# Gate and up of a gated layer: both pairs of token chunks by seven products in eight feature groups, instead of one pair

## The chip, the cores and the metric

The kernel runs on one core of a Trainium2 chip. Its engines have queues of their own and run side by side: TensorE (PE) multiplies into PSUM, VectorE (DVE), ScalarE (ACT) and GpSimd (POOL) work element by element, and SyncE (SP) issues DMAs. ACT and POOL can issue DMAs too. GpSimd reads and writes SBUF only. Each engine works through its instructions in the order in which the program gives them to it, and a waiting instruction holds up those behind it. The metric is the time of one execution on the device, in microseconds (us).

## The reference: what is computed

A sequence of 2048 tokens of width 640 is normalized; one branch is a dilated, sliding attention (32 heads of 20, 8 positions at distance 2), the other a bilinear gated layer with 1536 features, and their product is added to the input:

```
xn = layernorm(x)
s  = attention(xn @ wqkv) @ wo            # 8 keys per token: t, t-2, ..., t-14
h  = (xn @ w_gate) * (xn @ w_up)          # 640 -> 1536, twice
g  = silu(h @ w_down)                     # 1536 -> 640
out = x + s * g
```

The change is in the two products that make h.

## The kernel before, in words

**Precision.** Every matmul operand is split into a high part (rounded to the format that PE takes in one pass) and a low part (the rest). A product is then three passes: high x high, high x low, low x high (`ALL3`, line 109). A split is an ACT copy for the high part and a subtraction on POOL or DVE for the low part (`split`, line 104).

**Tiling.** The 2048 tokens are four chunks of 512 (`CH`); xT[c] holds chunk c transposed, as a high and a low tile of five blocks of 128 input features. The 1536 features of gate and up are twelve groups f of 128. gate_up (line 583) does one group for one chunk: 15 matmuls for gate, 15 for up, an ACT copy of gate, a DVE product h = gate x up, a store of h to DRAM (h_scr). Groups 0 and 1 are done this way for all chunks at the start, mixed with the first qkv products.

**Seven products.** For f = 2 to 11, `group(f)` (line 1215) takes chunks 0 and 1 together: gate and up of two chunks, over four of the five input blocks, are a 2 x 2 by 2 x 2 block product, done with seven block products instead of eight. It needs sums of weights (S1 to S4, made by `w_add` on POOL and split by `w_split`) and sums of activations (T1 to T4, made by `differences` on POOL during the qkv products). T4 takes the place of a part of xT[1]. The fifth input block is added by three matmuls each to four of the products (`FIVE`). That is 7 x 6 + 4 x 3 = 54 matmuls. Partial results are held by four ACT copies into the five-buffer tile gh (`hold`); DVE does gate_b, gate_a and up_a, POOL up_b and h_b. Chunks 2 and 3 are then done plainly (`gate`, `up`, `plain`): 60 matmuls, two ACT copies, two DVE products.

**Order of work.** The order in each engine's queue is the order of the calls, written out by hand. At the start (lines 1024 to 1104), tiles of 128 tokens are normalized on DVE: `moments_q` (batch statistics, line 315), `scales` (lines 322 to 328, a chain of small DVE operations on 128 x 4 elements), `spread` (a matmul on PE that stands in the middle of a gate_up, line 330), and `trans_q` (line 339): four applies (line 279), a 32 x 32 transpose (line 347), the high part on ACT (line 350) and the low part on DVE (line 351, put off by one tile). The qkv products of a tile (line 409) need its high and low parts. Attention is a Python generator (line 442): `advance` takes steps from it against a credit that each piece of PE work adds, so DVE and POOL instructions of attention are laid between those of the feature groups. Its products read one operand from PSUM (q_two and weights), its additions of terms run on POOL (line 482). `finish_piece` (line 623) lays the put-off DVE work of the last gate_up or group. begin_last (line 1350) lays all of attention that is left and loads wo; it comes in group 10. After group 11 the output projection and the down projection follow.

Of the kernel before, what the change touches and what calls it, by code (L numbers as in the profile page):

```python
# [19 lines left out]
P = 128  # L20
# [7 lines left out]
CH = 512  # L28
# [16 lines left out]
PACE = 1.0  # L45

# [7 lines left out]
def kernel(  # L54
# [174 lines left out]
    o_scr = dr.tile([DIL, NQ, NE, P, QC], F32, name="o_scr")  # L229
    h_scr = dr.tile([NT, P, KF, P], F32, name="h_scr")  # L230
# [124 lines left out]
    ORDER = [0, 1, 2, 3, 4, 6, 5, 7, 8, 10, 9, 11]  # L355
# [86 lines left out]
    def attention():  # L442
# [9 lines left out]
        before, late, loaded = None, [], set()  # L452
# [18 lines left out]
        def values(w):  # L471
# [5 lines left out]
            t = terms[:, w % 2, :NE * c] if w else y  # L477
# [4 lines left out]
            return NE * c * cost, lambda: eng.tensor_add(y, y, t)  # L482

        ring[:] = [q_one, "g", "u"]
        for n, u in enumerate(ORDER + [None]):
# [14 lines left out]
            for j in PAIRS:  # L500
# [6 lines left out]
                if before is not None:  # L507
                    cost, add = values(j or 1)
                    if j:
                        add()  # L510
                    else:
                        late.append(add)
                    yield cost
# [4 lines left out]
                if before is not None:  # L518
                    cost, add = values(j + 1 if j else 0)
                    if j:  # L520
                        add()
                    else:
                        late.pop()()
                    yield cost
# [23 lines left out]
            before = u, e, st([P, NE, c], "pk" if n in (7, 9, 11) else "o", 1)  # L548
# [13 lines left out]
    running = []  # L562

# [498 lines left out]
    low_parts()  # L1062
    finish_piece()
# [10 lines left out]
    gate_up(0, 1, amid=(lambda: spread(8),))  # L1074
    nc.scalar.activation(st([P, 1], "exp", 1), eps_t, AF.Exp)
# [3 lines left out]
    trans_q(10)  # L1079
    gate_up(1, 1, amid=(lambda: spread(12),))  # L1080
# [10 lines left out]
    trans_q(13)  # L1091
    trans_q(14)
    gate_up(0, 2)
    trans_q(15)
    low_parts()
    made.add(0)
# [10 lines left out]
    tt, tw, steps = [], {}, []  # L1107
# [3 lines left out]
    def t_unit(j, a, k):  # L1111

        if j == "T4":
            return xT[1][a][:, k, :]
        n, i = T_UNIT[j, a, k]
        while len(tt) <= n:
            tt.append(slot([P, 3, CH]))
        return tt[n][:, i]
# [3 lines left out]
    def differences(k):  # L1122
# [3 lines left out]

        def parts(j, y):
            nc.scalar.activation(t_unit(j, 0, k), y, AF.Copy)
            nc.gpsimd.tensor_sub(t_unit(j, 1, k), y, t_unit(j, 0, k).bitcast(F32))

        def minus(c, y):
            z = st([P, CH], "gh", 5)
            nc.gpsimd.tensor_sub(z, x(c[0], 0, c[1]), y)
            yield
            nc.gpsimd.tensor_add(z, z, x(c[0], 1, c[1]))
            yield
            return z

# [430 lines left out]
```

## Time and profile before

| what | value |
|---|---|
| median of 3 runs | 750.93 us (750.75 to 752.1) |
| the profiled execution | 750.62 us |
| its span, first to last instruction | 748.7 us |
| PE busy | 742.9 us, 4102 matmuls |
| DVE, POOL, ACT busy | 598.5, 423.8, 275.8 us |
| first matmul of group 2, of group 11 | 271.8, 504.4 us |

The span is shorter than the execution by what lies before the first and after the last instruction. Busy time counts instructions of an engine, not those that issue DMAs. A line such as "L279 DVE TENSOR_SCALAR" names the line of the kernel, the engine and the operation; "out<-in" gives the tiles. In the timeline a row has its start and its length in us, a count of merged instructions, and in brackets the idle time before it with what ended it. The granted clock of PE is 1.0 in nearly the whole span.

### The profile page before, as it was taken

The numbers are of one execution on the slowest core, as the hardware profiler recorded it, in microseconds if no ns is written. First come the engines' busy times: TensorE is split into PE (matmuls) and PEld (weight loads), VectorE is DVE, ScalarE is ACT, GpSimd is POOL, SyncE is SP. The second block draws the span as 40 slices with busy tenths as digits, with TensorE's granted clock in tenths as the row PEclk, the third lists the DMA queues.
The fourth block names the chain that finished last, engine by engine and source line by source line (L and its number), as shares of the span: only waits on it lengthen the run. The fifth ranks groups of instructions, "written<-read, shape, count | busy, mean of one in ns | idle before, by whom it ended". The sixth has DMA issues, their size and how long they took to land.

```text
span 748.7 us, 11061 instructions
## 1 busy us (share of the span) xinstructions
PE 742.9 (99%) x4102; PEld 678.5 (91%) x4102; DVE 598.5 (80%) x753; ACT 275.8 (37%) x513; POOL 423.8 (57%) x341
## 2 busy tenths in 40 slices
PE   9999999999999999999999999999999999999997
PEld 7989989988999998888888888888999999999997
DVE  7899897699687888978897887434998787777775
ACT  5334223232232332332232322235466564444442
POOL 6100329797698989895988798865659900000000
PEclk9999999999999999999999999999999999999999
DMA  9464352957627554636263522453667665555534
GB/s 330 155 201 118 119 167 81 280 179 231 178 84 224 181 169 129 205 92 186 76 183 88 154 63 56 146 159 91 175 186 214 210 237 190 190 190 190 190 106 141
DMA packets 99747, 122.48 MB, mean 164 GB/s; under 512 B 22280, under 2 KB 73988, under 8 KB 99694
## 3 DMA queue, kind: packets, MB, share of 16 engines
q1 hardware_dynamic: 82094, 107.53, 46.0%
q10 hardware_dynamic: 17600, 14.26, 5.9%
q8 instruction: 32, 0.52, 0.3%
q14 instruction: 21, 0.17, 0.1%
HBM read 78.34 MB, written 42.57 MB: 161 GB/s over the span
## 4 chain that ended last, share of the span: by engine, by line
PE 99%; DVE 0%; POOL 0%; ACT 0%; issue 0%; POOLq 0%
PE u L116 13%; PE g L116 13%; PE q L409 10%; PE q L852 8%; PE u L409 8%; PE g L1250 8%; PE g L409 8%; PE u L852 6%; PE u L1250 5%; PE g L852 3%; PE e L852 3%; PE q L1250 3%; PE q L116 2%; PE q L989 2%; PE u L989 1%; PE e L409 1%
## 5 line engine op out<-in xcount | busy, mean ns | idle before, releaser
L482 POOL TENSOR_TENSOR o<-o,t 128x960 f32<-128x960 f32 (+1 forms) x63 | 128.5, 2039 | 37.5 <-DVE o L479 26.4
L107 POOL TENSOR_TENSOR s<-wraw,s 128x640 fp32r<-128x640 f32 (+4 forms) x67 | 88.3, 1330 | 85.5 <-ACT s L106 82.6
L116 PE MATMUL g<-xc,s 128*128 128x512 f32 (+1 forms) x435 | 100.5, 382 | 0.0
L116 PE MATMUL u<-xc,s 128*128 128x512 f32 (+1 forms) x435 | 100.4, 382 | 0.0
L479 DVE TENSOR_TENSOR t<-e,kv 128x960 f32<-128x960 f32 (+1 forms) x84 | 87.1, 1038 | 13.6 <-POOL o L482 13.5
L505 DVE TENSOR_TENSOR t<-q,kv 128x1920 f32<-128x1920 f32 (+1 forms) x48 | 92.4, 1926 | 4.5 <-DMA kv<-qkv_scr 3.8
L116 PEld LDWEIGHTS u<-xc,s 128*128 128x128 f32 x435 | 79.7, 188 | 15.7
L116 PEld LDWEIGHTS g<-xc,s 128*128 128x128 f32 x435 | 79.7, 188 | 15.5
L515 DVE TENSOR_REDUCE lg<-t 128x96 f32<-128x1920 f32 (+1 forms) x48 | 92.3, 1923 | 0.1
L409 PE MATMUL q<-s,xc 128*128 128x360 f32 (+1 forms) x450 | 82.7, 334 | 0.0
L409 PEld LDWEIGHTS q<-s,xc 128*128 128x128 f32 x450 | 74.8, 188 | 4.0 <-POOL s L107 0.8
L409 PE MATMUL u<-s,xc 128*128 128x360 f32 (+1 forms) x360 | 65.8, 334 | 0.0
L409 PEld LDWEIGHTS u<-s,xc 128*128 128x128 f32 x360 | 60.3, 187 | 2.3
L409 PE MATMUL g<-s,xc 128*128 128x360 f32 (+1 forms) x330 | 61.5, 337 | 0.0
L106 ACT ACTIVATE s<-wraw 128x768 fp32r<-128x768 f32 (+6 forms) x68 | 41.9, 631 | 50.4 <-PE u L116 30.0
L409 PEld LDWEIGHTS g<-s,xc 128*128 128x128 f32 x330 | 55.7, 187 | 2.6
L852 PE MATMUL q<-xc,s 128*128 128x320 f32 x342 | 55.5, 309 | 0.0
L852 PEld LDWEIGHTS q<-xc,s 128*128 128x128 f32 x342 | 51.5, 188 | 0.0
L482 POOL TENSOR_TENSOR pk<-pk,t 128x960 f32<-128x960 f32 (+1 forms) x18 | 35.9, 1996 | 12.7 <-DVE pk L479 7.2
L1250 PE MATMUL g<-xc,s 128*128 128x512 f32 x150 | 37.3, 389 | 0.0
L815 DVE TENSOR_TENSOR s<-s,s 128x768 fp32r<-128x768 f32 x29 | 28.3, 975 | 10.1 <-ACT s L811 10.1
L1222 ACT ACTIVATE gh<-g 128x512 f32<-128x512 f32 x30 | 17.9, 598 | 46.2 <-PE g L1250 46.2
(341 smaller groups left out, 1342.5 us busy)
## 6 DMA issues: line engine op xcount, KB each, us to landing
h_scr<-gh SPq DMA_DIRECT2D x48, 256.0 KB, 2.5
wraw<-in_wgu SPq DMA_DIRECT2D x11, 640.0 KB, 4.6
kv<-qkv_scr SPq DMA_DIRECT2D x14, 480.0 KB, 5.1
qkv_scr<-s ACTq DMA_DIRECT2D x18, 360.0 KB, 3.3
t<-h_scr SPq DMA_DIRECT2D x8, 768.0 KB, 7.0
kv<-qkv_scr SPq DMA_DIRECT2D x14, 367.5 KB, 5.8
s_scr<-gh SPq DMA_DIRECT2D x16, 320.0 KB, 4.2
gh<-s_scr SPq DMA_DIRECT2D x16, 320.0 KB, 4.3
```

The costliest lines, as they stand in the source:

```text
L106: nc.scalar.activation(hi, raw, AF.Copy)
L107: eng.tensor_sub(lo, raw, hi.bitcast(F32))
L116: nc.tensor.matmul(acc, a, b, start=first and n == 0, stop=last and n == len(runs) - 1)
L409: nc.tensor.matmul(p, xT[(r * NE + i) // TPC][a][:, k, t0:t0 + P], wq[m][b][k], start=n == 0, stop=n == len(runs) - 1, skip_group_check=ac ...
L479: nc.vector.tensor_mul(t.rearrange("p (n d) -> p n d", d=DH), e[:, :, w].unsqueeze(2).to_broadcast([P, NE * nh, DH]), v)
L482: return NE * c * cost, lambda: eng.tensor_add(y, y, t)
L505: nc.vector.tensor_mul(t, q, k)
L515: nc.vector.tensor_reduce(out=lg[:, :, j:j + 2].rearrange("p n a -> p a n"), in_=t.rearrange("p a (n d) -> p a n d", d=DH), op=ALU.add, ax ...
L815: nc.vector.tensor_sub(hT[m][:, 1], h_raw[n][name], hT[m][:, 0].bitcast(F32))
L852: nc.tensor.matmul(p, y[:, i, k], wd_t[name][k][:, l], start=new and r == 0, stop=r == len(runs) - 1, skip_group_check=True)
L989: nc.tensor.matmul(b, y, w, start=new and r == 0, stop=r == len(runs) - 1, skip_group_check=True)
L1250: nc.tensor.matmul(y, w, x, start=j in (0, 1, 5) and r == 0, stop=r == len(runs) - 1, skip_group_check=True)
```

## The change

For f = 3 to 10 the second pair of chunks, now the pair 2 and 3 first and then 0 and 1, is done by seven products too, with the same sums of weights: `group(f, 2)` and `group(f, 0, 1)`. In f = 2 the seven products take pair 2/3 and the plain ones chunks 0 and 1; f = 11 stays as it was. For this:

- The sums T1 to T4 of pair 0/1 are made early. early_sums(0) stands after the qkv products of tiles 4 and 5, early_high(0) behind gate_up(0, 1), early_sums(1) after tile 10, early_high(1) after tile 13. Their tiles lie in buffers that held x; from there they go to DRAM (t_scr, e_scr). The part of xT[3] that T4 of pair 2/3 overwrites is kept in DRAM too.
- POOL's queue issues the loads: t_scr in groups 2 and 3, e_scr into xT[1] in group 3 and back into xT[3] after group 10.
- `differences` makes the sums of pair 2/3, in eleven POOL operations per k instead of thirteen.
- In the groups on pair 2/3 with f from 3 (VEC), up_b and h_b run on DVE instead of POOL; on pair 0/1 they stay on POOL. The splits and sums of the next group's weights are laid at given products of the second group (two_places). The up weights' first half (A21) is no longer split where no plain product needs it; the gate weights use the tile pk, so attention's results always use the tile o, and its first term goes to a tile of terms.
- The last rows of attention units run in the order 11, 9, 10, and the last qkv part takes r = 1 first.
- begin_last comes at the first product of group 10's second half; split_wo and sums_wo, which stood in group 10, come there and in group 11.

```
+    def early_sums(k):
+        r0, r1, a, b = early_t[:4]
...
+        for out, add, u, v in ((r0, 1, x(1, 0, 0), x(1, 1, 0)), (r1, 1, x(1, 0, 1), x(1, 1, 1)),
+                               (a, 0, r0, x(0, 0, 0)), (a, 0, a, x(0, 1, 0)), (b, 0, r1, a), (r0, 0, r1, r0),
+                               (r1, 0, x(0, 0, 1), b), (r1, 1, r1, x(0, 1, 1))):
+            (nc.gpsimd.tensor_add if add else nc.gpsimd.tensor_sub)(out, u, v)
+
+    def early_high(k):
+        r0, r1, a, b = early_t[:4]
+        for n, (j, y) in enumerate((("T1", a), ("T2", b), ("T3", r0), ("T4", r1))):
+            hi = early_t[4 + n].bitcast(F32R)
+            nc.scalar.activation(hi, y, AF.Copy)
+            nc.gpsimd.tensor_sub(y.bitcast(F32R), y, hi.bitcast(F32))
+            for l, t in enumerate((early_t[4 + n], y)):
+                nc.sync.dma_start(t_scr[:, T2_UNIT[j, l] + k] if j != "T4" else e_scr[l][:, k], t)
...
     qkv(0, 0, 4)
     qkv(0, 0, 5)
     low_parts()
+    early_sums(0)
     finish_piece()
     moments_q(8, 4)
...
     scales(12)
     gate_up(0, 1, amid=(lambda: spread(8),))
+    early_high(0)
     nc.scalar.activation(st([P, 1], "exp", 1), eps_t, AF.Exp)
     trans_q(8)
     trans_q(9)
     finish_piece()
     trans_q(10)
+    early_sums(1)
     gate_up(1, 1, amid=(lambda: spread(12),))
...
     trans_q(13)
+    early_high(1)
     trans_q(14)
     gate_up(0, 2)
     trans_q(15)
     low_parts()
+    for a in range(2):
+        nc.sync.dma_start(e_scr[2 + a], xT[3][a][:, 0:2, :].bitcast(F32))
...
-    def group(f):
+    def group(f, c0=0, second=0):
...
+        eng = nc.vector if c0 and f >= VEC else nc.gpsimd
...
         def up_b():
-            nc.gpsimd.tensor_add(kept[1], kept[1], kept[4])
+            eng.tensor_add(kept[1], kept[1], kept[4])
 
         def h_b():
-            nc.gpsimd.tensor_mul(kept[2], kept[2], kept[1])
-            store_h(f, 1, kept[2])
+            eng.tensor_mul(kept[2], kept[2], kept[1])
+            store_h(f, c0 + 1, kept[2])
...
+            if f < f1 and f + 1 not in wf_raw:
+                load_wf(f + 1)
...
+            if (second, n) in places:
+                places[second, n](f)
...
-            advance(PACE * len(runs) * 0.184)
+            advance(PACE * len(runs) * (GROUP_RATE if two(f) else 0.184))
...
+    beside.update({(f0, 1, 0): lambda: begin_last(), (f0, 1, 3): lambda: split_wo(0),
+                   (f1, 0, 1): lambda: (split_wo(1), sums_wo(), load_pair(1))})
...
+    two_places = {(0, 5): sums("S1"), (0, 6): sums("S2"), (1, 0): sums("S3"), (1, 1): sums("d5", "S4"),
+                  (1, 2): splits("G"), (1, 4): splits("S"), (1, 5): splits("R"), (1, 6): splits("U")}
...
     for f in range(2, f1):
...
+        places.clear()
+        if not two(f):
...
+            continue
+        places.update(two_places)
+        if f == F_TWO:
+            places.update({(0, n): lambda f, n=n: load_late(n) for n in range(4)})
+        group(f, 2)
+        group(f, 0, 1)
+    places.clear()
+    load_e(3, 0, 2)
+    load_e(3, 1, 3)
...
     group(f1)
```

Here VEC = 3, GROUP_RATE = 0.184 and F_TWO = 3; f0 is 10, f1 is 11, and two(f) is true for f = 3 to 10.

More of the change, by code (lines that the diff above doesn't have):

```diff
@@ L45 @@
 PACE = 1.0
+VEC = 3
+GROUP_RATE = 0.184
 def tile_column(s):
@@ L507, in attention @@
                 if before is not None:
[L508 to L512, printed above, removed]
+                    cost, add = values(j)
+                    add()
                     yield cost
```

191 lines of the change are left out of this document (109 added, 82 removed).

## The prediction

> **What bounds the kernel now.** I read the page first (busy shares, chain), then the windows for two stages, then single instructions in the timeline.
>
> ```profile
> span 748.7 us, 11061 instructions
> ...
> PE 742.9 (99%) x4102; PEld 678.5 (91%) x4102; DVE 598.5 (80%) x753; ACT 275.8 (37%) x513; POOL 423.8 (57%) x341
> ...
> PE 99%; DVE 0%; POOL 0%; ACT 0%; issue 0%; POOLq 0%
> ```
>
> TensorE (PE) is the bound from end to end: the chain that ended last is 99% PE. So a matmul that is removed is worth its whole pitch, and a wait that reaches PE anywhere costs its whole length. The profiled execution took 750.62 us, 1.92 us more than its span; the median of the runs is 750.93. I sum against 750.62. Differences under about 0.2% (1.5 us) can't be told from no change here.
>
> The windows show two stages that the change touches, [40, 60] and the feature groups f = 3 to 9 ([297.64, 478.52]; columns: length, then busy us of PE, PEld, DVE, ACT, POOL):
>
> ```profile
> 40.00:60.00 20.00, 20.00 (x103) 17.43 (x102) 18.81 (x60) 6.05 (x17) 0.00 (x0) 1.00 0.64 200
> ...
> 297.64:478.52 180.88, 180.88 (x799) 149.78 (x798) 149.69 (x141) 49.52 (x79) 153.16 (x113) 1.00 0.41 121
> ```
>
> In the first, VectorE (DVE) is 94% busy and GpSimd (POOL) idle; in the second DVE is at 83% and POOL at 85%.
>
> **Removed: 48 matmuls.** A feature group now costs PE 54 matmuls of 512 columns for the pair done by seven products and 60 for the two plain chunks. One turn of the loop is the time from one group's start to the next:
>
> ```profile
> 297.64 1.52 PE L1250 MATMUL g<-xc,s 128*128 128x512 f32 x6
> ...
> 323.48 0.84 PE L1250 MATMUL g<-xc,s 128*128 128x512 f32 x3
> ```
>
> That is 25.84 us for 114 matmuls, 0.2267 us each. For f = 3 to 10 the 60 become 54: 8 x 6 x 0.2267 = **10.9 us** less. A doubled turn is 108 x 0.2267 = 24.48 us. f = 2 and 11 keep their 114 (the pairs only swap in f = 2).
>
> **Added early: 24 POOL operations beside a full DVE.** early_sums has 8 operations of 512 columns per k, early_high 4 more (and 4 on ACT), for k = 0 and 1: 24 in all on POOL. The like of them, and POOL's idle time up to the split of the next weights, are
>
> ```profile
> 86.66 4.40 POOL L107 TENSOR_TENSOR s<-wraw,s 128x1080 fp32r<-128x1080 f32 x3 [60.05 <-ACT s L106]
> ...
> 109.52 1.29 POOL L1141 TENSOR_TENSOR gh<-xc,xc 128x512 f32<-128x512 f32 x1
> ```
>
> So 24 x 1.3 = 31 us fit into 60 us of idle POOL. By POOL's own time they are free. The question is what DVE does meanwhile. These rows are DVE operations with both inputs in SBUF, with POOL idle (507.28) and busy (526.56 and 528.27), and small ones and a normalization:
>
> ```profile
> 507.28 0.43 DVE L939 TENSOR_TENSOR kv<-kv,wraw 128x256 f32<-128x256 f32 x1
> ...
> 526.21 1.75 POOL L107 TENSOR_TENSOR xc<-o,xc 128x640 fp32r<-128x640 f32 x1
> 526.56 1.68 DVE L939 TENSOR_TENSOR t<-t,s 128x256 f32<-128x256 f32 x1
> ...
> 527.91 1.75 POOL L107 TENSOR_TENSOR s<-t,s 128x640 fp32r<-128x640 f32 x1
> 528.27 1.67 DVE L940 TENSOR_TENSOR t<-s,t 128x256 f32<-128x256 f32 x1
> ```
> ```profile
> 8.40 0.96 POOL L107 TENSOR_TENSOR s<-wraw,s 128x360 fp32r<-128x360 f32 x1
> ```
> ```profile
> 9.01 0.70 DVE L279 TENSOR_SCALAR t<-t,mv,r 128x640 f32<-128x640 f32 x1
> ...
> 17.26 0.61 DVE L279 TENSOR_SCALAR t<-t,mv,r 128x640 f32<-128x640 f32 x1
> ...
> 23.76 2.85 POOL L107 TENSOR_TENSOR s<-wraw,s 128x256 fp32r<-128x256 f32 x4
> ...
> 24.52 0.71 DVE L261 TENSOR_SCALAR lg<-mvo 128x4 f32<-128x4 f32 x1
> ...
> 25.34 0.58 DVE L273 TENSOR_TENSOR lg<-lg 128x4 f32<-128x4 f32 x1
> ```
>
> An operation of 0.43 us becomes 1.68: it ends 0.28 us after POOL's operation ends (526.21 + 1.75 = 527.96), and the next one waits for POOL's next. One DVE operation gets through per POOL operation. Even 4 columns take 0.71 instead of 0.17 us (the 0.17 is below, at 45.73). L279 with POOL in flight until 9.36 ends at 9.71, so its data seem to pass after POOL's end; uncovered, 640 columns take 0.61 us. So the applies, the low parts and the little tensor operations of the scales wait; batch statistics, 32x32 transposes and operations with an input in PSUM do not.
>
> The Trainium skill, page "SBUF — State Buffer", section "Who interferes with whom", says the same: GpSimd and VectorE share a port pair under an exclusive lock, a two-input operation in SBUF or a two-port mode needs it, and who comes second blocks for the whole instruction. By that rule, this trace agrees.
>
> *Stall A, at spread(8).* early_sums(0) can start when the low part of tile 7 ends (40.17 + 0.83 = 41.0):
>
> ```profile
> 40.17 0.83 DVE L351 TENSOR_TENSOR xc<-s,xc 128x640 fp32r<-128x640 f32 x1 [0.81 <-ACT xc L350]
> ...
> 45.73 0.17 DVE L261 TENSOR_SCALAR lg<-mvo 128x4 f32<-128x4 f32 x1
> ...
> 46.25 0.16 DVE L273 TENSOR_TENSOR lg<-lg 128x4 f32<-128x4 f32 x1
> 46.45 0.16 DVE L274 TENSOR_TENSOR lg<-lg 128x4 f32<-128x4 f32 x1
> ...
> 47.05 0.19 DVE L327 TENSOR_TENSOR lg<-mro,lg 128x32 f32<-128x32 f32 x1
> ```
> ```profile
> 44.01 3.56 PE L116 MATMUL g<-xc,s 128*128 128x512 f32 x15
> 47.40 0.36 PE L333 MATMUL e<-lg,lg 128*128 128x32 f32 x2
> ```
>
> Its eight operations end at about 41.0 + 8 x 1.29 = 51.3. scales(8) begins at 45.65, in the middle, and has five or more operations that wait (L261, L273, L274, L275, L276), one per POOL operation: they reach 51.3 before L327 runs, which so ends near 51.7 and not at 47.24. PE's spread (L333) stands in PE's queue between the gate and the up half and starts at 47.40, with no slack behind L327. PE stalls 51.8 - 47.4 = **4.4 us**.
>
> *Stall B, at tiles 8 to 11.* An ACT copy of 512 columns and a DMA issue on SP cost
>
> ```profile
> L1222 ACT ACTIVATE gh<-g 128x512 f32<-128x512 f32 x30 | 17.9, 598 | 46.2 <-PE g L1250 46.2
> ```
> ```profile
> L1212 SPq DMA_DIRECT2D h_scr<-gh x40: 359/376/534, 291.2 to 532.4; - x40
> ```
>
> Behind stall A ACT makes the four high parts of early_high(0) (4 x 0.6 us, ahead of the table load and of tile 8's copy), POOL its four low parts, then, once the store out of r0 has landed, early_sums(1). DVE meanwhile turns tiles 8 to 11 for the qkv products that PE does next (rows from 52.69: scales(12), a tile's applies, low part, transpose and high part, and PE's first four products of that row of tiles):
>
> ```profile
> 52.69 0.19 DVE L327 TENSOR_TENSOR lg<-mro,lg 128x32 f32<-128x32 f32 x1
> ...
> 57.91 1.16 DVE L279 TENSOR_SCALAR s<-s,lg 128x160 f32<-128x160 f32 x4
> 58.20 2.56 PE L409 MATMUL e<-s,xc 128*128 128x360 f32 x15
> 58.99 0.82 DVE L351 TENSOR_TENSOR xc<-s,xc 128x640 fp32r<-128x640 f32 x1
> 59.72 0.84 DVE L347 STREAM_TRANSPOSE s<-s 128x640 f32<-128x640 f32 x1
> 60.60 0.74 ACT L350 ACTIVATE xc<-s 128x640 fp32r<-128x640 f32 x1 [2.41 <-DVE s L347]
> 60.60 2.56 PE L409 MATMUL u<-s,xc 128*128 128x360 f32 x15
> ...
> 63.01 4.96 PE L409 MATMUL q<-s,xc 128*128 128x360 f32 x30
> ```
>
> A tile is four applies, a low part and a transpose, 2.8 us; PE takes a tile in 2.4 us and is 1 to 2 us behind. With POOL busy each apply costs one POOL operation (1.3 us), so a covered tile takes about 4 x 1.35 + 2 x 0.85 = 7 us. Walked through by that rule, from DVE free at 57.4 (scales(12), which ends at 52.9, 4.5 later): tile 8 is ready at 63.4 (PE wants it at 62.6), tile 9 at 66.2, the low part of 9 at 73.3 (wanted at 67.8), tile 10 at 75.0, tile 11 at 79.0; POOL's twelve operations are over at 76. The fourth product starts at 79.0 and not at 65.4 (63.0 + 2.4): 13.6 us late, of which 4.4 are stall A. **Stall B is 9.2 us.** Bounds: 0, and 12 x 1.2 = 14. I take the walk. The last four POOL operations (early_high(1), tiles 14 and 15) fall behind gate_up(0, 2), 6.8 us of PE work that needs none of them: 0.
>
> **Added in the doubled groups.** The plain chunks' two ACT copies and two DVE products become four ACT copies, three DVE operations, and an addition and a product (up_b, h_b) on POOL or, for pair 2/3 from f = 3 on (VEC), on DVE.
>
> ```profile
> L1225 DVE TENSOR_TENSOR gh<-gh,u 128x512 f32<-128x512 f32 x5 | 3.4, 683 | 4.7 <-PE u L1250 2.8 <-issue 1.9
> ```
> ```profile
> L1228 POOL TENSOR_TENSOR gh<-gh,gh 128x512 f32<-128x512 f32 x5 | 6.5, 1294 | 0.0
> ```
> ```profile
> 478.90 2.27 POOL L482 TENSOR_TENSOR pk<-pk,t 128x960 f32<-128x960 f32 x1 [2.16 <-DVE t L479]
> ```
>
> DVE today: 149.69 / 7 = 21.4 us a turn, of which 5 x 0.68 = 3.4 are the groups' and 18.0 attention's. The pacing gives attention 108 x 0.184 = 19.9 credits a turn against 54 x 0.184 + 4 x 2.8 = 21.1, so 16.9 us. New: 16.9 + 6 x 0.68 + two operations with both inputs in SBUF, 0.7 each plus a wait of some 0.9 behind a POOL that is 85% busy = 24.2 us of 24.48. DVE is full. With half a microsecond of waits a turn it falls behind by some tenths per turn, for six turns, until attention ends; the five gh buffers (a hold needs the store of the group before it to have landed) pass a lag beyond some 3 us on to PE. I take **2 us**; bounds 0 and, if DVE holds a turn at the old length, 6 x 1.36 = 8.2. POOL stays near 85%; its weight splits are now due within a few products of the last use, which is in the same bound. ACT, 7 us a turn, has room for 1.2 more.
>
> **At nothing.** The 26 new DMAs (18 on SP, 8 on POOL) meet DMA engines 41% busy (the share in the window above) and are needed 10 us or more after issue; if late, the first product on T2 waits a few us, once. On SP the early stores wait for POOL, and behind them stand the h stores of two gate_up calls (five gh buffers, two used per call) and the load of the next qkv weights, which are split at 85: covered. POOL issues eight loads, an operation that no row here shows: between 0 and SP's issue time, 0.38 us each. The Trainium skill, "DMA: Bandwidth & Descriptors", section "SWDGE vs HWDGE vs iDMA", has GpSimd's DMAs built in software; no run here shows a price. Attention keeps its number of products and additions; two POOL operations per k fall away from differences, off the path. At the end attention is over at 481.2 (478.90 + 2.27, its last POOL addition) and begin_last comes near 482.6, then wo has 5.4 us to land: 0, at most 2.
>
> **Sum.** 750.6 - 10.9 + 4.4 + 9.2 + 2.0 = **755.3 us**.
>
> **Rivals.** (1) *The early work hides* (faster). If POOL's operations let the short DVE operations pass, or run where DVE has statistics and transposes, the early stalls shrink. Decisive is what one POOL operation costs the path: 13.6 us are 18 or so operations at 0.75 us; under (10.9 - 2) / 18 = 0.5 us each the kernel wins. For it: the statistics before 45 us don't wait. Against: no DVE slack there, 18.81 of 20 us. With stall A alone 746.1; with neither 741.7. (2) *DVE bounds the doubled groups*: their gain is lost until attention ends, and wo is late: 755.3 + 6.2 + 2 = 763. (3) *The change does not save what it says*: matmuls with a longer pitch from reloaded tiles. Against: all 512-column forms have the same 0.2267. I give it nothing.
>
> **How the numbers follow.** Forecast 0.56 (751 to 759); rival 1 0.30, of which 0.05 within 0.2% as partial hiding; rival 2 0.10; the rest 0.04 on the line. Faster 0.25, same 0.09, slower 0.66. Low end 742, rival 1 with neither stall; high end 763, rival 2; some 0.2 is left out.
>
> **What would show it.** PE: 4054 matmuls; gaps before L333 near 47 us and before the qkv products of tiles 8 to 11; applies of 1.3 us with POOL beside them; a turn of 24.5 to 25 us in the doubled groups, with up_b and h_b on DVE at 1 to 2 us. Wrong if applies keep 0.3 us each beside POOL, or if PE has no gap before 80 us.

## The result, and the profile after

The changed kernel takes 760.24 us (median of 4, 758.93 to 762.56), the kernel before 750.94 beside it (4, 750.75 to 752.1): a ratio of 1.0124, 95% interval 1.0097 to 1.0151. It is 9.3 us slower. The profiled execution took 760.15 us. From its page: the span, the busy times, and the shares of the chain that ended last:

```profile
span 758.4 us, 11100 instructions
...
PE 739.7 (98%) x4054; PEld 673.3 (89%) x4054; DVE 633.9 (84%) x777; ACT 286.3 (38%) x537; POOL 452.0 (60%) x369
...
PE 70%; DVE 12%; POOL 8%; DMA 5%; issue 4%; ACT 1%; SPq 0%; ACTq 0%; DVEq 0%; POOLq 0%
```

PE has its 48 matmuls fewer, but the chain is no longer PE alone: 30% of it is other engines and transfers, so PE now waits. (A share of the chain is not a share of waiting: PE is still busy 98% of the span.) The list of PE's waits says for whom (sum, times, longest):

```profile
PE u L413 <- DVE xc L355: 4.2, 1, 4.2
PE g L1304 <- ACT gh L1271: 3.1, 3, 1.5
PE e L337 <- DVE lg L331: 3.0, 1, 3.0
PE e L1017 <- DVE xc L996: 1.4, 1, 1.4
```

The first and third are the two early stalls of the prediction; the second are holds that wait for a gh buffer, once each in f = 4, 6 and 11; the fourth stands in the output projection. The windows for the first of the stages shown of before, for f = 3 to 10, and for f = 11 and the start of the output projection:

```profile
40.00:60.00 20.00, 17.02 (x78) 14.43 (x78) 18.70 (x46) 6.94 (x19) 13.79 (x11) 0.91 0.68 217
309.50:508.50 199.00, 197.09 (x866) 161.86 (x865) 171.88 (x172) 63.46 (x106) 167.59 (x128) 1.00 0.48 141
508.50:546.00 37.50, 34.35 (x168) 29.02 (x167) 30.79 (x37) 16.15 (x28) 28.44 (x22) 1.00 0.64 171
```

A doubled turn is 24.48 us where nothing waits (four of the eight), as forecast, so eight turns should save 8 x (25.84 - 24.48) = 10.9 us. I cut every run into three parts by the starts of its matmuls: **early** is how much later f = 2 starts than in the kernel before (after: 283.66 against 271.80), **doubled** is what the eight turns take over 195.8 us, **end** is what all that follows takes over the kernel before. The profiled execution's time against that of before (750.62) is -10.9 plus the three, within 0.2. "Time" is the median where there were several rounds (the marked ones), else the profiled execution; for e16 and e18 the profiled ones took 749.62 and 748.39. Six of the kernels (after, e6, e7, e10, e12, e14) have the same code up to f = 2 and lose 11.9 to 13.5 us there, so a difference of 1.6 us between two single executions says little.

| run | early | doubled | end | time |
|---|---|---|---|---|
| after (4 runs) | 11.9 | 3.1 | 5.4 | 760.24 |
| e1_no_pool | 0.5 | 2.9 | 4.4 | 747.56 |
| e2_memset | 8.9 | 2.0 | 4.5 | 755.47 |
| e4_paced | 11.5 | 2.8 | 6.6 | 760.78 |
| e5_paced2 | 13.1 | 2.4 | 4.8 | 760.45 |
| e6_load_e | 13.5 | 2.6 | 7.3 | 763.13 |
| e7_act_store | 13.1 | 17.0 | 2.7 | 772.67 |
| e8_all (4 runs) | 11.0 | 15.2 | 4.8 | 771.81 |
| e9_paced3 (4 runs) | 15.2 | 3.8 | 4.8 | 763.57 |
| e10_const_h | 12.7 | 0.6 | 5.2 | 758.70 |
| e11_paced3_const_h | 15.2 | 0.6 | 5.5 | 761.12 |
| e12_no_load_e | 12.4 | 2.7 | 5.0 | 759.88 |
| e13_paced4 | 3.7 | 2.3 | 4.7 | 750.83 |
| e14_end | 12.1 | 18.8 | 4.9 | 775.71 |
| e15_both (4 runs) | 3.3 | 17.9 | 4.6 | 766.82 |
| e16_f10_dve (11 runs) | 3.9 | 1.6 | 4.4 | 750.73 |
| e17_all_dve (4 runs) | 3.6 | 7.6 | 4.6 | 755.65 |
| e18_sums_late (11 runs) | 3.2 | 2.3 | 3.1 | 750.01 |

### The profile page after: what moved, and what is told of

It reads as the page before. It is cut to its first block, busy times and chain, and to the rows that moved or that the text cites. A ratio compares the mean times of both kernels' runs of the same rounds, so it can differ in the third digit from the quotient of the medians.

```text
span 758.4 us, 11100 instructions
## 1 busy us (share of the span) xinstructions
PE 739.7 (98%) x4054; PEld 673.3 (89%) x4054; DVE 633.9 (84%) x777; ACT 286.3 (38%) x537; POOL 452.0 (60%) x369
## 4 chain that ended last, share of the span: by engine, by line
PE 70%; DVE 12%; POOL 8%; DMA 5%; issue 4%; ACT 1%; SPq 0%; ACTq 0%; DVEq 0%; POOLq 0%
PE g L1304 11%; PE q L880 8%; PE q L413 6%; PE u L1304 6%; PE u L880 6%; PE u L413 5%; PE g L413 4%; POOL o L489 4%; PE q L1304 3%; PE g L118 3%; PE g L880 3%; PE e L880 3%; DMA h_scr<-gh 3%; PE q L118 2%; PE u L118 2%
## 5 line engine op out<-in xcount | busy, mean ns | idle before, releaser
L483 DVE TENSOR_TENSOR t<-e,kv 128x960 f32<-128x960 f32 (+1 forms) x96 | 99.4, 1037 | 23.9 <-POOL o L489 23.8
L109 POOL TENSOR_TENSOR s<-wraw,s 128x384 fp32r<-128x384 f32 (+6 forms) x58 | 68.8, 1195 | 27.2 <-ACT s L108 27.1
L1271 ACT ACTIVATE gh<-g 128x512 f32<-128x512 f32 x54 | 32.3, 598 | 118.3 <-PE g L1304 100.6
L1304 PE MATMUL u<-xc,s 128*128 128x512 f32 x216 | 55.0, 390 | 0.3 <-ACT gh L1271 0.3
L1304 PE MATMUL g<-s,s 128*128 128x512 f32 x216 | 54.8, 389 | 0.0
L1304 PEld LDWEIGHTS u<-xc,s 128*128 128x128 f32 x216 | 40.5, 188 | 9.1 <-ACT gh L1271 0.7
L1304 PEld LDWEIGHTS g<-s,s 128*128 128x128 f32 x216 | 40.5, 188 | 8.4
L489 POOL TENSOR_TENSOR o<-t 128x960 f32<-128x960 f32 (+1 forms) x12 | 24.8, 2063 | 37.4 <-DVE t L483 26.7
L108 ACT ACTIVATE s<-wraw 128x384 fp32r<-128x384 f32 (+6 forms) x59 | 33.4, 587 | 28.8 <-PE g L1304 9.1
L118 PE MATMUL u<-xc,s 128*128 128x512 f32 (+1 forms) x180 | 41.6, 383 | 0.0
```

The lines of the kernel that those rows point to most:

```text
L108: nc.scalar.activation(hi, raw, AF.Copy)
L109: eng.tensor_sub(lo, raw, hi.bitcast(F32))
L118: nc.tensor.matmul(acc, a, b, start=first and n == 0, stop=last and n == len(runs) - 1)
L483: nc.vector.tensor_mul(t.rearrange("p (n d) -> p n d", d=DH), e[:, :, w].unsqueeze(2).to_broadcast([P, NE * nh, DH]), v)
L489: return NE * c * cost, lambda: eng.tensor_add(y, z, t)
L1271: nc.scalar.activation(kept[j], b["ACACABA"[j]], AF.Copy)
```

## Experiments

**The early loss: who makes it.** In the kernel after, scales(8) and the tiles of stall B look like this (DVE from the timeline):

```profile
45.94 0.62 DVE L328 COPY mro<-mvo 128x4 f32<-128x4 f32 x1
...
46.74 1.17 DVE L277 TENSOR_TENSOR lg<-lg 128x4 f32<-128x4 f32 x1
47.95 1.19 DVE L278 TENSOR_TENSOR lg<-lg 128x4 f32<-128x4 f32 x1
49.17 0.17 DVE L279 TENSOR_SCALAR lg<-lg 128x4 f32<-128x4 f32 x1
49.37 1.10 DVE L280 TENSOR_TENSOR mro<-lg 128x4 f32<-128x4 f32 x1
...
61.18 1.27 DVE L283 TENSOR_SCALAR pk<-pk,lg 128x160 f32<-128x160 f32 x4
...
64.44 5.37 DVE L283 TENSOR_SCALAR s<-s,lg 128x160 f32<-128x160 f32 x4
69.73 1.88 DVE L355 TENSOR_TENSOR xc<-s,xc 128x640 fp32r<-128x640 f32 x1
```

Four operations of the scales take 4.1 us and not 0.65; four applies 5.37 us with POOL busy and 1.27 where it rests. What the prediction left out of the waits does not wait: beside a busy POOL statistics take 0.83 us (at 43.83), a 32x32 transpose 0.83 (71.54) and a product with one operand in PSUM 0.65 (63.87), as in the kernel before beside an idle one (0.83, 0.84 and 0.65). Three runs ask whether POOL's operations are the cause, and by which of their accesses.

e1_no_pool: in early_sums `pass` stands for the POOL operation; in early_high

```
-            nc.scalar.activation(hi, y, AF.Copy)
-            nc.gpsimd.tensor_sub(y.bitcast(F32R), y, hi.bitcast(F32))
+            nc.scalar.activation(hi, xT[1][0][:, n % 2, :].bitcast(F32), AF.Copy)
```

> The kernel after without the 24 early operations on POOL (8 sums and 4 low parts for each k); ACT's eight early copies and the 16 early stores stay, with other data, so T1 to T4 of the first pair are not computed. Theory 1 (these POOL operations hold up DVE, and through it PE): both early stalls go, the first product of group f = 2 starts 0 to 0.5 us behind that of the kernel before instead of 11.9, and the time is 760.2 - 11.6 = 748.6 us. Rival (the copies on ACT, the stores on SP's queue or the DMA cost it): the start of f = 2 stays 8 us or more late and the time 757 or more. Both: the 8.5 us lost from f = 3 to the end stay as they are.

Measured: early 0.5, all of it in the first 10 us, and 747.56 us. The stores, and copies that wait for no POOL operation, cost nothing here; the POOL operations cost all of it, directly or through what waits for them.

e2_memset:

```
-            (nc.gpsimd.tensor_add if add else nc.gpsimd.tensor_sub)(out, u, v)
+            flat = xc.rearrange("p a b -> p (a b)")
+            nc.gpsimd.memset(flat[:, 618:2048] if out is r1 else flat[:, :1430], 0.0)
...
-            nc.gpsimd.tensor_sub(y.bitcast(F32R), y, hi.bitcast(F32))
+            for c in (CH, CH, CH // 2):
+                nc.gpsimd.memset(y[:, :c], 0.0)
```

> The kernel after with each early POOL operation replaced by POOL memsets that take about as long (1430 columns at 0.84 ns and 0.09 us make 1.29 us; three for a low part), which write SBUF and read nothing; T1 to T4 of the first pair are not computed. Theory 1 in its narrow form (only POOL's reads stand against DVE's second input): no early stall, f = 2 starts 0 to 0.5 us late, 748.6 us. Theory 1 in its wide form (operations with two SBUF inputs wait for POOL's reads alone, but the applies, which run at two columns a cycle over both ports, wait for its writes as well): the scales pass, so stall A goes (-4.8), and the applies of tiles 8 to 11 still wait, so most of stall B stays (4 to 7 us): f = 2 starts 4 to 7 us late, 753 to 756 us. Rival (a busy POOL as such, its semaphores or its instruction queue, delays others): both stalls stay, 760 us.

Measured: 755.47 us, early 8.9: the wide form, with more left than its 4 to 7, and PE still waits 1.4 us at the spread. A part of that is the edit's own: the first two memsets wait for no sum and start at 37.0 and 40.8 us (the first sums at 41.4), so tile 7's applies are 1 us late already. Its DVE rows in the timeline:

```profile
47.62 0.16 DVE L277 TENSOR_TENSOR lg<-lg 128x4 f32<-128x4 f32 x1
...
48.01 0.89 DVE L279 TENSOR_SCALAR lg<-lg 128x4 f32<-128x4 f32 x1
...
64.62 4.66 DVE L283 TENSOR_SCALAR s<-s,lg 128x160 f32<-128x160 f32 x4
69.20 0.80 DVE L355 TENSOR_TENSOR xc<-s,xc 128x640 fp32r<-128x640 f32 x1
```

Beside a POOL that only writes (memsets run from 40.81 to 50.22 and from 63.84 to 74.57), operations with two tensors pass (L277 0.16, the low part 0.80 where the kernel after has 1.17 and 1.88), and those with one tensor and scalars still wait. So two kinds of DVE operation wait for two different things. The Trainium skill, "SBUF — State Buffer", section "Who interferes with whom", draws the same line: a second SBUF input stands against GpSimd's reads alone, a two-port mode against any access. These rows agree.

e3_before_early: the functions early_sums and early_high, their DRAM tiles and the four calls, added to the kernel before.

> The kernel before with nothing added but the early work of the first pair (24 operations on POOL, 8 copies on ACT, 16 stores to DRAM) at the places where the kernel after has it; nothing reads what it stores. Theory 1: the early loss comes from this alone, f = 2 starts 11 to 12 us late and stays so, 750.6 + 11.6 = 762.2 us. Rival (the loss needs something else of the change: the order of the units, the additions of attention, the later groups): less than 8 us, under 759.

Measured: 762.54 us, f = 2 starts 12.1 us late and the lateness stays to the end. The early loss is complete without any other part of the change.

**Is the price moved or removed?** Four kernels keep all the early work and place it otherwise.

e4_paced (behind(y) is a one-column POOL copy that waits for y):

```
+    early_sums(0, 0, 3)
...
     scales(8)
+    behind(own[8][:, 0, 0, 0:1])
+    early_sums(0, 3, 6)
...
     trans_q(11)
+    behind(turned[0][:, 1, 0, 0:1])
+    early_sums(0, 6, 8)
+    early_high(0)
...
     trans_q(15)
     low_parts()
+    behind(xT[3][1][:, 0, CH - 1:].bitcast(F32))
+    early_sums(1)
+    early_high(1)
```

> The kernel after with the same 24 POOL operations at other times: three of the first sums beside the statistics of tiles 8 to 11, three more held back until scales(8) is through, beside the statistics of tiles 12 to 15, the last two sums and the four low parts of k = 0 held back until tile 11 has been turned, and all of k = 1 until tile 15 is done (two small copies more on POOL hold them back, and a third for k = 1). Theory 1: statistics do not wait, and tiles 12 to 15 have 5 to 8 us to spare (tile 12 was ready at 66.4 and wanted at 74.6 in the kernel before), so both stalls go: f = 2 starts 0 to 2 us late, 748.6 to 751 us. Rival (the POOL operations cost PE their time wherever they stand, or the copies and stores do): f = 2 starts 8 us or more late, 757 or more.

Measured: 760.78, early 11.5. Both stalls were gone (no wait from 10 to 66 us), but PE then had two others:

```profile
PE u L118 <- ACT pk L426: 5.1, 1, 5.1
...
PE q L413 <- DVE xc L355: 2.1, 1, 2.1
```

The first is an order on ACT: the early copies wait for POOL's sums and hold up the evictions behind them. The second is tile 11's low part, held up by POOL started one step too soon.

e5_paced2 mends both: the hold-back of k = 0 is on the low part of tile 11, early_high(0) stands behind trans_q(13), early_high(1) behind the four qkv products, attention's first advance behind that.

> As e4_paced, with its two new waits taken away: the last two sums of k = 0 are held back until the low part of tile 11 is done (not only its turn), the high and low parts of k = 0 stand behind tile 13, and those of k = 1 stand behind the products of tiles 12 to 15 in ACT's queue, so that no eviction waits behind a copy that waits for POOL; attention's first steps stand behind them. Same 24 operations, copies and stores. Theory 1 (only what a POOL operation blocks at its moment costs): f = 2 starts 0 to 1.5 us late, 748.5 to 750 us, the 8.5 us behind it unchanged. Rival (the early work has a price that is only moved about): f = 2 starts 6 us or more late, 755 or more.

Measured: no wait of PE from 10 to 94 us, then one of 7.0 us; early 13.1, 760.45. Its DVE:

```profile
92.16 2.16 DVE L512 TENSOR_TENSOR t<-q,kv 128x1920 f32<-128x1920 f32 x1 [7.03 <-ACT q L473]
...
100.87 0.68 DVE L637 TENSOR_TENSOR gh<-u,gh 128x512 f32<-128x512 f32 x1
```

VectorE stands idle until ACT has copied q behind the early copies, and the product that frees PE's bank (L637) stands behind attention.

e9_paced3 hands out attention's first budget after gate_up(1, 3).

> As e5_paced2, which had no wait of PE before 94 us but then one of 7.0 us: the release of a bank by DVE (the product of a gate_up piece) stood behind attention's first operations, which waited for ACT's copy of q, which stood behind the early copies. Here attention's first budget is handed out after the first two features instead of during the products of tiles 12 to 15, so that DVE's product stands ahead of it. Theory 1: f = 2 starts 0 to 2 us late, the losses behind it stay at 7 to 9 us, 747.5 to 751 us: as fast as the kernel before or a little faster. Rival (the early work has a price that is only moved about, because POOL and DVE have no room left until f = 2): f = 2 starts 6 us or more late, 755 us or more.

Measured: 763.57 (ratio 1.0166, 1.0149 to 1.0183), early 15.2: from 10 to 101 us PE has no wait, then evictions wait on ACT behind an exponential of a late attention and behind copies of late differences (8.6 us, three times). The rival seemed right.

e13_paced4 takes away only what e5's rows show:

```
+    ring[:] = [q_one, "g", "u"]
     for i in range(TPC, NE):
         qkv(0, 1, i)
+        if i == TPC:
+            q0 = q_t[0].rearrange("p i c -> p (i c)")
+            nc.scalar.activation(q_two[:, :q0.shape[1]], q0, AF.Copy)
+    early_high(1)
+    split_wq(1, nc.gpsimd)
+    advance(PACE * 1.9 * TPC)
```

> As e5_paced2, with ACT's copy of the first unit's q made ahead of the early copies of k = 1 (during the products of tiles 12 to 15), and the split of the next weights ahead of attention's first steps on POOL. Theory 1 (each wait has its own cause, here an order on ACT): VectorE starts attention near 84 us, PE has no wait over 1 us until f = 2, which starts 0 to 2 us late: 747.5 to 751 us. Rival (the early work takes time that VectorE and POOL do not have before f = 2): f = 2 starts 6 us or more late, 754 or more.

Measured: 750.83 us, early 3.7. DVE starts at once:

```profile
80.54 2.16 DVE L512 TENSOR_TENSOR t<-q,kv 128x1920 f32<-128x1920 f32 x1 [0.27 <-ACT q L1141]
```

and PE has no wait over 0.7 us between 10 and 397 us. So most of the price of the early work was that of its places: 8.2 of 11.9 us went with the same 24 operations. The 3.7 left are more than the 0 to 2 expected (last section).

**The doubled turns and the end.** First the hold that waits in the kernel after, in f = 6 (ACT and SP from the timeline, then the DMA issues from 394 to 412 us: KB each, median us from issue to landing):

```profile
407.64 0.60 ACT L1271 ACTIVATE gh<-g 128x512 f32<-128x512 f32 x1 [3.53 <-DMA h_scr<-gh]
```
```profile
399.39 0.91 SPq L401 DMA_DIRECT2D kv<-qkv_scr  x2
400.40 0.94 SPq L1260 DMA_DIRECT2D h_scr<-gh  x2
```
```profile
h_scr<-gh SPq DMA_DIRECT2D x2, 256.0 KB, 7.3
...
kv<-qkv_scr SPq DMA_DIRECT2D x1, 480.0 KB, 8.1
```

The buffer is still being stored, behind attention's loads (7.3 us to landing, where the median of all stores of h is 2.4). In f = 11 the same hold waits 3.55 us for a store whose product came late, because POOL had an addition, a weight split and two loads in front of it:

```profile
509.61 1.28 POOL L1277 TENSOR_TENSOR gh<-gh,gh 128x512 f32<-128x512 f32 x1
510.86 1.55 POOL L109 TENSOR_TENSOR s<-wraw,s 128x640 fp32r<-128x640 f32 x1
512.37 1.14 POOL L1162 DMA_DIRECT2D xc<-e_scr  x2
513.51 1.31 POOL L1280 TENSOR_TENSOR gh<-gh,gh 128x512 f32<-128x512 f32 x1
```

e6_load_e: the two calls of load_e moved into `beside[f0, 1, 1]`.

> The kernel after with only the two loads that bring the fourth chunk's parts back (issued by POOL, 1.14 us together, ahead of the last addition and product of f = 10) moved one group earlier, into the second group of f = 10. Theory 2 (these issues delay POOL's product h_b, so its store, so the gh buffer that the next hold takes; and the lateness is carried to the waits near 544 us): the wait of f = 11 (1.8 us) goes and the tail's 3.6 us too, 760.2 - 5.4 = 754.8 us. Rival (the store lands late because DMA engines are busy, and the tail's waits have another cause): 758 to 760 us.

Measured: 763.13, end 7.3, more than without the edit. A miss: POOL was free for h_b, but the first pair's load landed late beside them, and ACT's hold waited behind that pair's high part (DVE's turn of the pair):

```profile
517.10 1.57 DVE L694 STREAM_TRANSPOSE wraw<-kv 128x640 f32<-128x640 f32 x2 [6.63 <-DMA kv<-o_scr]
```

e12_no_load_e: the two calls left out.

> The kernel after without the two loads that bring back the fourth chunk's parts ahead of the group f = 11 (1.14 us of POOL, 1 MB), so that the last plain products of that chunk take differences in place of its parts and the output is not the reference's. Theory 2 as it stood before e6_load_e (these loads delay POOL, and they and the pair's loads share the DMA engines): the wait in f = 11 (1.8 us) and the tail (3.6) go, 754.8 us. Rival (the end of the doubled groups is late by itself, as POOL has its weight splits and h_b to do there): 758 us or more.

Measured: 759.88. The store lands in 3.1 us and not 4.8, the wait in f = 11 falls under 0.3, but 0.5 at the release of a bank and 1.9 at the output projection stand there; end 5.0. The loads are not the cause of the end's loss.

e7_act_store: `eng = nc.scalar if two(f) else nc.sync` for the store of h.

> The kernel after with only the h stores of f = 3 to 10 issued from ACT's queue and not from SP's, where attention's stores and loads stand ahead of them. Theory 2 (the waits of f = 3 to 6 are for gh buffers whose stores land late behind attention's transfers): the 3.1 us of waits in f = 3, 4 and 6 shrink to under 1, 757 us; ACT issues some 32 stores of about 0.5 us, 2 us a turn on an engine that is a third busy. Rival (the theory on record: VectorE is full in these turns, and the buffers are late because of it): the waits stay, 760 us.

Measured: 772.67, doubled 17.0. A miss: on ACT the store waits for POOL's h_b, and the next hold stands behind it (ACT of that run):

```profile
344.05 0.93 ACTq L1261 DMA_DIRECT2D h_scr<-gh  x2
345.08 0.60 ACT L1272 ACTIVATE gh<-g 128x512 f32<-128x512 f32 x1 [6.80 <-issue]
```

e8_all was e5, e6 and e7 in one.

> The kernel after with the changes of e5_paced2, e6_load_e and e7_act_store together. If each gain is its own: f = 2 starts 0 to 1.5 us late, the waits behind it are under 2 us, and the time is 750.6 - 10.9 + 1 to 3 = 741 to 743 us, faster than both kernels. If the waits of the doubled groups only move to the next resource (VectorE or POOL, both at 85%): 745 to 750 us.

Measured: 771.81 (1.0288, 1.027 to 1.0305): the early wait of e5 (7.05 us), the doubled turns of e7.

e10_const_h:

```
-                          y.rearrange("p (t c) -> p t c", c=P))
+                          (xT[0][0][:, KD - 1, :].bitcast(F32) if two(f) else y).rearrange("p (t c) -> p t c", c=P))
```

> The kernel after with the h stores of f = 3 to 10 taking their data from a tile that always stands (one row of the first chunk) and not from the gh buffer: the same stores, but a gh buffer is free as soon as VectorE or POOL is done with it; the h of these features is wrong in DRAM, so the output is not the reference's. Theory 2 (the waits of the doubled groups are for stores of h that have not landed): the waits of f = 3, 4 and 6 (3.1 us) fall under 0.5, that of f = 11 (1.8) too, and the tail's 3.6 with it if it follows from that: 751.7 us, or 755.3 without the tail. Rival (the theory on record: VectorE full, so late with the sums that the holds wait for): the turns stay as long, 760 us.

Measured: 758.70. Doubled falls from 3.1 to 0.6: those waits were for stores. (In the doubled turns ACT's holds waited 13.1 us for them in the kernel after, seven times; here never.) The end keeps 5.2; its hold no longer waits, and others come out:

```profile
PE e L1017 <- DVE xc L996: 1.9, 1, 1.9
...
PE g L118 <- DVE gh L1287: 1.2, 1, 1.2
```

VectorE is behind there as well. e11_paced3_const_h put this beside e9.

> e9_paced3 and e10_const_h together: early work that does not hold up PE, and buffers that do not wait for stores (same wrong h in DRAM). If both theories hold, nearly the whole of the 10.9 us that the removed matmuls are worth is there: 740 to 744 us. Rival (losses behind f = 2 come from VectorE or POOL being full): 746 us or more.

Measured: 761.12, early 15.2 from e9, doubled 0.6: the two parts add.

e14_end:

```
-GROUP_RATE = 0.184
+GROUP_RATE = 0.1955
...
+    beside.update({(f0, 0, 4): lambda: begin_last(), (f0, 1, 0): lambda: split_wo(0),
+                   (f0, 1, 3): lambda: (split_wo(1), sums_wo()), (f0, 1, 6): lambda: load_pair(1)})
```

> The kernel after with the work for the output projection at the places of the kernel before (the loads in the first group of f = 10 and not in its second, the first split at the start of the second group, the second split and the sums of wo in its middle, the second pair's load at its end), and attention paced at 0.1955 per product in the doubled turns, so that a turn hands out 21.1 as before and not 19.9. Theory 3 (f = 11 waits because this work was put half a turn later): f = 11 and the stage behind it lose under 1.5 us and not 4.3, 756 to 757.5 us. Rival A (VectorE full, the theory on record): the turns of f = 3 to 9 grow by 0.5 us or more each, 762 us or more. Rival B (POOL and VectorE have less time beside a shorter turn and are late at the end wherever this work stands): the loss at the end stays, 759 to 761 us.

Measured: 775.71. The time is rival A's, the cause is not. The turns of f = 3, 5, 7 and 10 grow by 1.3 to 2.1 us and that of f = 9 by 11.5, but VectorE is 87% busy in the first 199 us of them (172.6), and what it and ACT wait for is POOL: its late h_b (a hold in f = 5), and in f = 9 its first addition of the last unit, which waits for the store of the only tile o:

```profile
369.17 0.60 ACT L1271 ACTIVATE gh<-u 128x512 f32<-128x512 f32 x1 [3.57 <-POOL gh L1280]
```
```profile
480.35 2.25 POOL L489 TENSOR_TENSOR o<-t 128x960 f32<-128x960 f32 x1 [8.80 <-DMA o_scr<-o]
```

The sums of wo are out of f = 11 here, and the end loses 4.9 all the same, to the hold that waits for the store: theory 3 alone does not explain it. e15_both:

> e13_paced4 and e14_end together. If both theories hold: f = 2 starts 0 to 2 us late, 3 us of waits for gh buffers stay in f = 3 to 6, the end loses under 1.5: 739.7 + 3 to 6.5 = 743 to 746 us, faster than both kernels. If the early price is only moved: 753 us or more.

Measured: 766.82 (1.0218, 1.0201 to 1.0235), early 3.3, the rest as e14.

e16_f10_dve, on top of e13 (e17_all_dve has `eng = nc.vector if two(f) else nc.gpsimd` in its place):

```
-        eng = nc.vector if c0 and f >= VEC else nc.gpsimd
+        eng = nc.vector if f >= VEC and (c0 or f == f0) else nc.gpsimd
...
-                   (f1, 0, 1): lambda: (split_wo(1), sums_wo(), load_pair(1))})
+                   (f1, 0, 1): lambda: (split_wo(1), load_pair(1))})
...
-    beside.update({(f1, 0, 0): lambda: turn_pair(0),
+    beside.update({(f1, 0, 0): lambda: (sums_wo(), turn_pair(0)),
```

> e13_paced4 with two things moved at the end of the loop: the addition and the product of h_b of the second group of f = 10 on VectorE and not on POOL, and the sums of wo one product earlier, ahead of the first pair's turn, where VectorE stands idle. Theory (the hold in f = 11 waits for a store that POOL issues late): the wait of 2.5 us in f = 11 and about 0.9 us of half clock behind it go, 747 to 748.5 us, faster than the kernel before. Rival (behind it VectorE or the DMA engines are late as well, as when e6_load_e moved the loads): the wait goes and another of 1.5 to 3 us comes at the end of f = 11 or at the output projection, 749.5 to 751 us.

Measured: 750.73 (1.000, 0.9991 to 1.0009), end 4.4. The wait for the store went, and the rival's came: ACT's hold stands behind the first pair's high part, which waits for VectorE, which makes the sums of wo first, the first two of them beside POOL splits:

```profile
501.75 1.59 DVE L920 TENSOR_TENSOR kv<-t 128x640 f32<-128x640 f32 x1
503.27 2.77 DVE L921 TENSOR_TENSOR kv<-t,t 128x640 f32<-128x640 f32 x1
...
507.61 1.56 DVE L694 STREAM_TRANSPOSE wraw<-kv 128x640 f32<-128x640 f32 x2
```
```profile
508.48 0.74 ACT L992 ACTIVATE kv<-wraw 128x640 fp32r<-128x640 f32 x1 [3.90 <-DVE wraw L694]
509.12 0.58 ACT L1280 ACTIVATE gh<-u 128x512 f32<-128x512 f32 x1
```

> e16_f10_dve with the addition and the product of h_b on VectorE in all groups of f = 3 to 10. If VectorE has room (86% busy in these turns in the kernel after, 3.4 us idle a turn, of which this takes 1.4 to 2.7): the gh buffers come free earlier and the waits of f = 3 to 6 shrink by 1 to 2 us, 745.5 to 747.5. If VectorE is full, as the prediction on record had it: the turns grow by 0.3 us or more each until attention ends, 749 us or more.

Measured: 755.65 (1.0068, 1.0054 to 1.0082), doubled 7.6. The windows for eight turns, e17 and then e13:

```profile
298.00:497.00 199.00, 194.76 (x849) 159.84 (x848) 189.12 (x187) 58.83 (x99) 149.79 (x110) 0.99 0.44 131
```
```profile
298.20:496.40 198.20, 196.81 (x866) 161.97 (x865) 173.46 (x173) 61.43 (x103) 166.96 (x129) 1.00 0.47 138
```

With VectorE at 95% the turns are 5.2 us longer than at 88%, some 1.6 of it half clock behind a wait in f = 7 (last section); two of the late holds stand behind an exponential that waits 2.3 and 2.6 us for VectorE. This is what a full VectorE looks like, and the kernel after (86%) is below it.

e18_sums_late: h_b of f = 10 on VectorE as in e16, and `(f1, 0, 3): lambda: (sums_wo(), load_pair(1))`.

> e13_paced4 with the addition and the product of h_b of the second group of f = 10 on VectorE, as in e16_f10_dve, but with the sums of wo (and the second pair's load behind them) two products later than in the kernel after, behind the first pair's turn and first low part. Theory (an order: whatever stands ahead of a hold on ACT or of its buffer's release makes it late): f = 11 has no wait over 0.5 us, 747 to 748.5 us, faster than the kernel before. Rival (VectorE has no room at the end of the loop): a wait of 1.5 us or more in f = 11 or at the output projection, 749.5 us or more.

Measured: 750.01 us against 750.89, a ratio of 0.9989 (0.998 to 0.9998), 1.3% below the kernel after and about 0.1% below the kernel before. f = 11 has no wait left, but the rival's 1.9 us stand at the output projection, and the median is the rival's too. The end of 3.1 needs care: it is that of the profiled execution, at 748.39 the fastest of eleven and 1.6 us under their median. The windows from the start of f = 11 on, e16 and then e18 (granted clock: third column from the end):

```profile
499.00:545.00 46.00, 43.59 (x223) 38.17 (x222) 38.19 (x50) 20.97 (x40) 30.04 (x23) 0.96 0.61 167
```
```profile
499.00:545.00 46.00, 43.80 (x231) 38.31 (x230) 41.36 (x52) 21.57 (x41) 31.20 (x24) 1.00 0.61 167
```

PE waits 2.4 us in the first and 2.1 in the second; most of the difference of 1.3 between their ends is a stretch of half clock that this execution of e18 does not have. In six of the eleven the mean granted clock is 0.997 or 0.998 and not 0.999, as one such stretch makes it, and those took 749.8 to 750.64, the other five 748.39 to 750.01. So the edit removed the wait in f = 11; that it made the end as a whole shorter is not shown. By its median it is the fastest of the versions that leave nothing out.

## Why the prediction was right or wrong

1. *48 matmuls, 10.9 us.* Right: 4054 matmuls, turns of 24.48 us.
2. *Stall A, 4.4.* Right in place and cause: PE waits 3.0 us at the spread (in the list above), and f = 2's lateness grows by 4.8 there. Four operations waited and not five or more, so the wait is shorter; half clock behind it, not forecast, adds 1.6 (last section).
3. *Stall B, 9.2.* Right in place and cause, 6.8 measured (wait 4.2, the rest half clock and smaller waits). The walk had POOL busy without a break. In fact it rested 4.5 us for ACT's copies and 1.7 for a store:

```profile
56.38 1.39 POOL L586 TENSOR_TENSOR kv<-kv 128x512 fp32r<-128x512 f32 x1 [4.53 <-ACT kv L585]
...
63.24 2.54 POOL L578 TENSOR_TENSOR kv<-xc 128x512 f32<-128x512 f32 x2 [1.71 <-DMA t_scr<-kv]
```

   and one tile passed uncovered at 61.18. The early sum was 13.6, measured 11.9 (4.8, 6.8 and 0.3 in the first 10 us): 1.7 less. That it came so near is in part luck: 13.6 were all waits, and of the 11.9 some 3.3 are half clock, for which the prediction has no term.
4. *Added in the doubled groups, 2.0.* Near in size, 3.1, but by another mechanism. VectorE was not full: 86% busy, up_b and h_b at 1.10 and 0.87 us and not 1.6, and with stores that hold no buffer 0.6 is left (e10). The stores landed late, in f = 6 behind attention's loads on SP's queue; no run moves those loads alone, so that part of the cause is read from the rows and not tested. e17 shows what a full VectorE costs.
5. *"At nothing", with the end "0, at most 2".* **This is the step that failed**: 5.4 us. The prediction counted one transfer of what moved to the end of the loop, and put it at 482.6 us; the loads of wo come in the second half of f = 10, and with them one of two splits on POOL (at 514.8 us; the other at 505.3) and four sums on VectorE move into f = 11. The term has no half clock either: of the 5.4 us, 1.8 are lost at the hold in f = 11 and 3.6 at the output projection, where PE waits 1.7 and nearly all the rest is half clock. The sums of wo before, and after:

```profile
491.57 0.82 DVE L892 TENSOR_TENSOR kv<-t 128x640 f32<-128x640 f32 x1
```
```profile
517.80 0.82 DVE L920 TENSOR_TENSOR kv<-t 128x640 f32<-128x640 f32 x1
```

   Before, they began 12.8 us ahead of f = 11 (504.36), beside plain products; after, 9.3 us behind its start (508.47), where the stores of h out of five gh buffers, h_b on POOL and the first pair's turn are due as well. Whichever of these is eased, the next is late: the end loses 4.4 to 5.5 us in fourteen of the table's eighteen rows, wherever PE happens to wait. That the figure is so steady is in part the clock: every row but those of e7, e9 and e18 has one stretch of half clock in its end, some 1.6 us, beside waits of 2.3 to 4.7. (e7 has the least, 2.7, behind a turn of f = 10 that was 2 us longer.) e10, e12, e14 and e16, which each ease one, show that no single one of them makes the loss, and e14, which put this work back to its old places, still lost 4.9. So the runs show that the term was not nothing and where PE waits; that the moved work makes these waits is argued. Which share each part has, and how to remove them, stays open.
6. *POOL's issue of a load, between 0 and 0.38 us.* Wrong: 1.14 us for two, 0.54 to 0.60 for one.

Sum: -10.9 + 11.9 + 3.1 + 5.4 = +9.5, measured +9.3; the forecast was +4.7. Stalls and direction stood; the error is the end, and the 1.7 too much early and the 1.1 too little in the doubled turns cancel in part. Rival 1 (the early work hides) was wrong of this kernel and turned out possible for the most part: in e13, by other places, 8.2 of the 11.9 us are hidden.

## What to carry to other kernels

Work put "into idle GpSimd time" is paid by VectorE where its operations read two SBUF tensors, or are copies and applies of one SBUF tensor as here: place it beside statistics, transposes and operations on PSUM, and look at the copies and evictions that then queue behind it on ScalarE. When a change fills the loop's last turn, list every instruction that used to run there, with the buffers it shares, and not only the transfers. A stall that moves when one cause is eased is not yet explained: measure the stage as a whole, and look at the granted clock before you credit an edit with a gain of 1 to 2 us.

## Unexpected of the hardware

Behind some waits of PE its granted clock is half for 3.4 us. Windows of the kernel after behind the waits at 47 and 67 us and those near 543 to 546 us (granted clock: third column from the end):

```profile
51.80:55.20 3.40, 3.40 (x9) 2.62 (x9) 3.11 (x12) 0.39 (x3) 0.05 (x1) 0.51 0.26 39
72.30:75.70 3.40, 3.22 (x11) 2.75 (x11) 3.40 (x7) 1.31 (x3) 1.73 (x2) 0.51 0.02 5
546.70:550.10 3.40, 3.40 (x15) 3.40 (x14) 1.71 (x4) 1.57 (x4) 0.00 (x0) 0.50 0.45 141
```

The clock is back after that; each time about 1.6 us are lost beyond the wait. The Trainium skill, "TensorE: Matmul & The Clock Gate", section "Part 1: The HAM clock gate", has the half clock after an idle window of some 3.4 us. Here less was enough: one wait of 3.0 us, of 2.4 (f = 11 in e16), and waits of 1.4 and 0.2 us close together. In e18 waits of 1.9 and 0.2 us at that same place left the clock whole, and behind the 7.0 us of e5 it was half for 6.8; no run here says what decides. And in e13, e16 and e18 (in e5, e11, e15 and e17 too) fifteen products of 360 columns take 2.63 us from some 150 us to f = 2, not 2.56, with full clock: 4 ns each, some 2 of the 3.7 us that e13's early part still loses. No run here says why.

```profile
211.32 2.63 PE L413 MATMUL u<-s,xc 128*128 128x360 f32 x15
```
